# Loading queries, keys and values of the first eight attention tiles in fewer, longer transfers, with a planner that counts the places for transfers

## The chip, the cores and the metric

The kernel runs on one core of a Trainium2 chip. The metric is device time in microseconds (us), from one launch. Before the change, three runs took 1085.28, 1087.08 and 1091.06 us; the median is 1087.08 us. A profile was taken of one further execution.

The engines are named as in the profile: PE is the matrix engine (PEld its weight loads), DVE the vector engine, ACT the scalar engine, POOL the GpSimd engine and SP the one that issues most DMA transfers.

## The reference

Chunked attention over 4 batches, 8 heads, 768 tokens and 64 dimensions is followed by two feed-forward layers over the same 3072 tokens.

```python
# attention: 24 chunks of 32 queries; keys are 16 before, the chunk, 8 after, and 8 memory keys
k_full = np.concatenate([mem_k, k_ctx], axis=2)
v_full = np.concatenate([mem_v, v_ctx], axis=2)
scores = scale * np.matmul(q_c, k_full.transpose(0, 1, 3, 2))
a = np.exp(scores - np.max(scores, axis=-1, keepdims=True))
a = a / (np.sum(a, axis=-1, keepdims=True) + 1e-09)
out[:, :, c_start:c_end] = np.matmul(a, v_full)

# layer 1 on x [3072, 512], w_in [512, 2048], w_out [2048, 512]
h = x @ w_in
g = np.maximum(h, 0.0) + np.log1p(np.exp(-np.abs(h)))
x = (g @ w_out).astype(np.float32)
# layer 2, the same shapes
h = x @ w_in
g = np.maximum(h, 0.0) + alpha * np.minimum(h, 0.0)
out = (g @ w_out).astype(np.float32)
```

The weights come in as 64-bit floats (in_w_dram) and are made into 32-bit ones on the chip.

## The kernel before

**The tiles.** Attention is cut into 24 tiles of 128 tokens with all 8 heads. For a tile, the host lays out one block of 128 rows and 1664 floats: 1024 floats of Q, in which each head's 64 columns stand beside 64 zeros for the other head of the pair, and 640 floats of K (4 head pairs of 160 keys; the 8 memory keys stand at place 88 of each 160). Another block holds V as 96 rows of two halves of 512 floats.

**A block of work of layer 1** is either `h i` (12 matrix products of 128x512, which give one 128-wide slice of the hidden layer for 512 tokens) or `out i` (12 products which add that slice into the layer's output). The 512 tokens of four tiles are one batch b. Step i has a batch and a slice f; steps 0 to 3 are batch 0 with slices 0 to 3, steps 4 to 7 batch 1 with the same slices, and new slices begin again with step 8. So h 0 needs tiles 0 to 3, and h 4 needs tiles 4 to 7.

**The first eight tiles** (numbers 0 to 7, `t < 2 * TB`) are computed before and between the first blocks. One tile goes through: load Q and K (`load_q` twice, `load_k`), copy the memory keys to both ends of K on POOL (`a_mem`, name `km`), scores on PE (`a_scores`, name `s`, 32 small products), maximum, shift and exponent (`m`, `c`, `e`), sum, reciprocal and share (`n`, `r`, `w`), transpose on PE (`t`), copies on ACT (`pt`), values on PE (`v*`, 16 products), and a split of the result in two parts for exact products (`xh` on ACT, `xl` on DVE). For tile t, V is loaded by `load_v` in six transfers: two halves of 512 floats, each in pieces of 8, 56 and 64 rows.

**The weights** come as transfers `raw n` of 512 KB into three buffers. Five DVE instructions (`ab`, `cl`, `ca`, `cb`, `cv`) turn one into 32-bit floats; `wh` on ACT and `wl` on DVE split it in two parts. Slice f needs two of them.

**The order.** A planner (class `Plan`) takes each piece of work with an engine, a cost in us, a due time and what it comes after, and lays them out on all engines in one pass; the program is then written out in that order, and each engine does its instructions in that order. In the kernel before, the order of the opening is also written out by hand (`OPENING`), and due times come from a table of numbers `O`. A transfer costs the planner its issue on SP, its time on one resource "DMA" and 1.4 us more until its data may be used. All SP transfers go through eight places that are taken in turn: each transfer's issue waits until the one eight before it has landed.

**Filler.** `keep_busy` puts products with a tile of zeros into PE's queue ahead of a piece for which the planner sees PE wait early in the run; they change nothing in the result. The first of them fill the time before the first scores.

Of the kernel before, what the change touches and what calls it, by code (L numbers as in the profile page):

```python
# [35 lines left out]

VLATER = (
# [30 lines left out]
class InOrder:  # L68
# [5 lines left out]
    def __getattr__(self, name):  # L74
# [17 lines left out]
OPENING = {
    "": """
        qr 0, qr 1, qr 2, qr 3, vr 0, vr 1, vr 2, vr 3, qr 4, qr 5, vr 4, qr 6, vr 5, qr 7, vr 6, vr 7, qr 8, vr 8
    """,
    "DVE": """
        corners, m 0, c 0, m 1, n 0, c 1, r 0, w 0, n 1, r 1, m 2, w 1, c 2, ab 0, m 3, cl 0, c 3, n 2, ca 0, r 2, cb 0, w 2, ab 1, n 3, xl 0, r 3, cl
        1, w 3, cv 0, ca 1, ab 2, cb 1, wl 0, xl 2, cv 1, cl 2, ca 2, wl 2, cb 2, cv 2, xl 1, wl 1, xl 3, m 4, c 4, ab 3, cl 3, n 4, ca 3, r 4, cb 3,
        ab 4, lo 0, cv 3, lo 1, m 5, wl 4, c 5, ab 5, cl 4, cl 5, ca 4, cb 4, n 5, xl 4, r 5, cv 4, m 6, ca 5, c 6, cb 5, wl 3, n 6, cv 5, r 6, m 7, c
        7, wl 6, ab 6, cl 6, ca 6, cb 6, n 7, lo 2, r 7, cv 6, xl 5, wl 5, ab 7, cl 7, ca 7, cb 7, ab 8, cv 7, cl 8, xl 6, lo 3, wl 8, xl 7, ca 8, ab  # L100
        9, cb 8, cl 9, cv 8, ab 10, ca 9, cl 10, cb 9, wl 7, cv 9, lo 4, ca 10, wl 10
    """,
    "SP": """
        i q 0 0, i q 1 0, i q 0 1, i q 1 1, i qk 0 2, i qk 1 2, i cst, i q 2 0, i q 3 0, i q 2 1, i q 3 1, i qk 2 2, i qk 3 2, i v 2, i raw 0, i v 0,
        i raw 1, i v 3, i raw 2, i v 1, i q 4 0, i q 4 1, i qk 4 2, i q 5 0, i v 4, i q 5 1, i raw 3, i qk 5 2, i raw 4, i q 6 0, i v 5, i q 6 1, i
        raw 5, i qk 6 2, i q 7 0, i v 6, i q 7 1, i qk 7 2, i v 7, i raw 6, i q 8 0, i q 8 1, i qk 8 2, i v 8, i raw 7, i raw 8, i raw 9, i raw 10, i
        raw 11, i raw 12
    """,
    "POOL": """
        km 0, km 1, km 2, km 3, km 4, km 5, w 4, km 6, w 5, km 7, w 6, km 8, w 7  # L110
    """,
    "PE": """
        s 0, s 1, s 2, t 0, s 3, t 1, v* 0, t 2, v* 2, t 3, v* 1, v* 3, s 4, h 0, h 1, s 5, t 4, out 0, v* 4, s 6, h 2, s 7, t 5, out 1, t 6, v* 5, h
        3, v* 6, t 7, out 2, v* 7, h 4, h 5, out 3
    """,
    "ACT": """
# [6 lines left out]
class Plan:  # L123
# [18 lines left out]
    def run(self):  # L142
# [12 lines left out]
        while left:  # L155
            able = []
            for name, since in ready.items():
# [4 lines left out]
                if engine == "SP":  # L162
                    t = max(t, free.get("DMA", 0.0) - 4.0)
# [1104 lines left out]
```

## Time and profile before

| | us |
|---|---|
| runs: median (lowest to highest) | 1087.08 (1085.28 to 1091.06) |
| the profiled execution, whole | 1090.2 |
| its span, first to last instruction | 1088.1 |
| PE busy in the span | 1066.2 |
| DVE busy | 704.4 |
| ACT busy | 543.1 |
| POOL busy | 171.8 |

The profiled execution is 3.1 us above the median of the runs, and 2.1 us of it lie outside the span. An engine's busy time is the union of its instructions; a busy PE can be at either of its two clocks. A timeline row gives the start and the duration of instructions that follow each other with the same line, operation and tiles, and in brackets how long the engine stood idle before them and what released it. All helpers are recorded at line 76, so rows are told apart by their tiles.

### The profile page before, as it was taken

The numbers are of one execution on the slowest core, as the hardware profiler recorded it, in microseconds if no ns is written. First come the engines' busy times: TensorE is split into PE (matmuls) and PEld (weight loads), VectorE is DVE, ScalarE is ACT, GpSimd is POOL, SyncE is SP. The second block draws the span as 40 slices with busy tenths as digits, with TensorE's granted clock in tenths as the row PEclk, the third lists the DMA queues.
The fourth block names the chain that finished last, engine by engine and source line by source line (L and its number), as shares of the span: only waits on it lengthen the run. The fifth ranks groups of instructions, "written<-read, shape, count | busy, mean of one in ns | idle before, by whom it ended". The sixth has DMA issues, their size and how long they took to land.

```text
span 1088.1 us, 18751 instructions
## 1 busy us (share of the span) xinstructions
PE 1066.2 (98%) x7281; PEld 871.0 (80%) x7281; DVE 704.4 (65%) x1182; ACT 543.1 (50%) x940; POOL 171.8 (16%) x213
## 2 busy tenths in 40 slices
PE   6799999999999999999999999999999999999998
PEld 4568888778888888888888888888888888888886
DVE  5789988655554564345455156678666779566976
ACT  4564435455453454444344255664555755456643
POOL 0010112434234233222323100000000010000000
PEclk9989999999999999999999999999999999999999
DMA  8885674767656564535355173799875999856904
GB/s 203 209 188 182 188 196 126 187 184 192 197 165 183 175 170 128 187 120 166 111 180 191 61 288 126 282 282 322 200 280 174 327 298 256 259 203 256 372 0 78
DMA packets 156441, 214.69 MB, mean 197 GB/s; under 512 B 78656, under 2 KB 108480, under 8 KB 149440
## 3 DMA queue, kind: packets, MB, share of 16 engines
q1 hardware_dynamic: 152048, 196.58, 56.9%
q0 software_dynamic: 4032, 16.78, 8.1%
q8 instruction: 57, 0.93, 0.4%
q14 instruction: 32, 0.26, 0.1%
q10 hardware_dynamic: 272, 0.13, 0.0%
HBM read 154.74 MB, written 46.14 MB: 185 GB/s over the span
## 4 chain that ended last, share of the span: by engine, by line
PE 92%; DMA 5%; SPq 2%; DVE 1%; issue 0%; DVEq 0%
PE ps_q L76 42%; PE ps_hh L76 23%; PE ps_o L76 23%; PE ps_a L76 3%; DMA raw<-in_w_dram 3%; SPq L76 2%; DMA v<-in_v_dram 1%; DVE word L76 1%; DMA qk<-in_qk_dram 0%; DVE x L76 0%; DVE g L76 0%; DVE sm L76 0%; DVE wsplit L76 0%; DVE v L76 0%; DVE c L76 0%
## 5 line engine op out<-in xcount | busy, mean ns | idle before, releaser
L76 PE MATMUL ps_hh<-x,wsplit 128*128 128x512 f32 x1152 | 282.5, 394 | 1.9 <-DVE x L76 1.1
L76 PE MATMUL ps_o<-g,wsplit 128*128 128x512 f32 x1152 | 280.4, 392 | 0.8 <-DVE g L76 0.8
L76 PEld LDWEIGHTS ps_hh<-x,wsplit 128*128 128x128 f32 x1152 | 216.7, 189 | 49.0 <-DVE x L76 1.6
L76 PEld LDWEIGHTS ps_o<-g,wsplit 128*128 128x128 f32 x1152 | 214.3, 188 | 46.0 <-DVE g L76 1.1
L76 PE MATMUL ps_q<-xop,win 128*128 128x512 f32 x1008 | 229.1, 389 | 0.0
L76 PE MATMUL ps_q<-g,wout 128*128 128x512 f32 x1008 | 229.1, 389 | 0.0
L76 PEld LDWEIGHTS ps_q<-g,wout 128*128 128x128 f32 x1008 | 189.0, 188 | 39.5
L76 PEld LDWEIGHTS ps_q<-xop,win 128*128 128x128 f32 x1008 | 189.2, 188 | 39.3
L76 DVE TENSOR_TENSOR g<-ta,g 128x512 fp32r<-128x512 f32 x96 | 70.9, 738 | 132.5 <-ACT g L76 132.2
L76 ACT CAST g<-gb 128x512 fp32r<-128x512 f32 x168 | 100.8, 622 | 89.8 <-PE ps_q L76 66.1
L76 DVE TENSOR_TENSOR g<-gb,g 128x512 fp32r<-128x512 f32 x168 | 114.2, 686 | 35.2 <-ACT g L76 33.2
L76 ACT CAST g<-ta 128x512 fp32r<-128x512 f32 x96 | 59.6, 621 | 120.8 <-PE ps_o L76 120.6
L76 ACT ACTIVATE ta<-ps_hh 128x512 f32<-128x512 f32 x96 | 57.5, 599 | 119.8 <-PE ps_hh L76 116.5
L76 DVE SCALAR_TENSOR_TENSOR word<-raw,word 128x512 int32<-128x512 int32 x128 | 91.5, 715 | 2.7
L76 ACT ACTIVATE tp<-gb 128x512 f32<-128x512 f32 x48 | 30.4, 633 | 91.4 <-DVE gb L76 91.4
L76 POOL TENSOR_TENSOR wst<-wsum,wst 128x512 fp32r<-128x512 f32 x32 | 45.0, 1406 | 127.0 <-ACT wst L76 121.3
L76 DVE SCALAR_TENSOR_TENSOR gb<-gb,tp 128x512 f32<-128x512 f32 x48 | 33.2, 692 | 44.0 <-ACT tp L76 44.0
L76 DVE TENSOR_SCALAR word<-word 128x512 f32<-128x512 f32 (+1 forms) x128 | 57.3, 452 | 2.1
L76 POOL TENSOR_TENSOR wst<-word,wst 128x512 fp32r<-128x512 f32 (+1 forms) x32 | 34.2, 1068 | 140.3 <-ACT wst L76 135.1
L76 DVE TENSOR_SCALAR word<-raw 128x512 int32<-128x512 int32 x64 | 30.0, 471 | 39.8 <-DMA raw<-in_w_dram 26.9
L76 ACT ACT_TABLE_LOAD x38 | 48.8, 1283 | 11.1 <-DVE nm L76 10.5
L76 POOL DMA_DIRECT2D gb<-gb x12 | 10.4, 864 | 277.3 <-DVE g L76 168.4
(87 smaller groups left out, 860.6 us busy)
## 6 DMA issues: line engine op xcount, KB each, us to landing
wout<-out_ops SPq DMA_DIRECT2D x42, 1024.0 KB
raw<-in_w_dram SPq DMA_DIRECT2D x64, 512.0 KB
win<-in_ops SPq DMA_DIRECT2D x24, 1024.0 KB
win<-in_ops SPq DMA_DIRECT2D x24, 768.0 KB
out_ops<-wst SPq DMA_DIRECT2D x56, 256.0 KB
in_ops<-wst SPq DMA_DIRECT2D x24, 512.0 KB
gb<-gb POOLq DMA_DIRECT2D x12, 1024.0 KB, 13.7
qk<-in_qk_dram SPq DMA_DIRECT2D x24, 320.0 KB
```

Of the source, the lines that this page charges most:

```text
L76: i = getattr(self.engine, name)(*args, **kw)
```

## The change

Q and K of tiles 0 to 7 are loaded as whole rows of 1664 floats by one transfer in place of three (the zeros are then loaded too). V of these tiles is loaded by six transfers in two groups of three: 56 rows of both halves at once (runs of 4 KB), and twice 8 rows of one half. The order of the V rows in a tile changes with it. The memory keys are no longer copied; instead, for the first and the last chunk of a tile, `a_scores` makes two products in place of one, one of 56 keys and one of the 8 memory keys, so that a tile has 48 small products in place of 32.

In the planner, the written order `OPENING` is gone, as is the rule that SP runs at most 4 us ahead of the DMA. Each SP transfer takes one to four of eight places ("lane"), which come back when it has landed. Many costs are set anew, the wait after a transfer is 1.8 us, and work that follows work on the same engine starts 0.02 us after it rather than 0.15 us. The table `O` has other numbers, and `keep_busy` fills nine tenths of a wait, less 0.2 us, where it filled six tenths, less 0.5 us.

```diff
+FEW = KW - NMEM
+WINDOWS = (((0, 0, FEW), (FEW, MEM0, NMEM)), ((0, CHUNK, KW),), ((0, 2 * CHUNK, KW),), ((0, MEM0, NMEM), (NMEM, KT - FEW, FEW)))
+VFIRST = (
+    ((0, FEW, 0, None), (FEW, NMEM, MEM0, 0), (FEW, NMEM, FEW, 1)),
+    ((D + NMEM, FEW, SW - FEW, None), (D, NMEM, CHUNK, 0), (D, NMEM, MEM0 - D, 1)),
+)
...
-OPENING = {
...
-                if engine == "SP":
-                    t = max(t, free.get("DMA", 0.0) - 4.0)
...
-                if t < 90.0 and t - free.get("PE", 0.0) > 0.5:
+                if t < 90.0 and t - free.get("PE", 0.0) > 0.4:
...
-                    ready[a] = max(done[b] for b in left[a][4]) + self.LAG
+                    e = left[a][0]
+                    ready[a] = max(done[b] + (0.02 if e and e != "DMA" and self.pieces[b][0] == e else self.LAG) for b in left[a][4])
...
+    def load_rows(t):
+        sp.dma_start(out=rows_of[t][:, :QK], in_=qk[t])
...
-    def load_v(t):
+    def load_v(t, h):
         if t < 2 * TB:
-            for u, to, at, n in (
-                (0, 0, MEM0, NMEM), (0, NMEM, 0, KW - NMEM), (0, KW, CHUNK, KW),
-                (1, 0, 0, KW), (1, KW, SW - KW + NMEM, KW - NMEM), (1, 2 * KW - NMEM, MEM0 - D, NMEM),
-            ):
-                part = slice(u * DM, (u + 1) * DM)
-                sp.dma_start(out=v_t[t][to:to + n, part], in_=v[t][at:at + n, part])
+            for to, many, at, u in VFIRST[h]:
+                part = slice(0, 2 * DM) if u is None else slice(u * DM, (u + 1) * DM)
+                sp.dma_start(out=v_t[t][to:to + many, part], in_=v[t][at:at + many, part])
...
-                        pe.matmul(
-                            ps[at:at + CHUNK, g, u, :], lhsT=q[rows, u * NPAIR + g, c * CHUNK:(c + 1) * CHUNK],
-                            rhs=k_t[t][rows, g, KEYS[j]:KEYS[j] + KW], start=True, stop=True,
-                        )
+                        for to, key, many in WINDOWS[j]:
+                            pe.matmul(
+                                ps[at:at + CHUNK, g, u, to:to + many], lhsT=q[rows, u * NPAIR + g, e, c * CHUNK:(c + 1) * CHUNK],
+                                rhs=k_t[t][rows, g, key:key + many], start=True, stop=True,
+                            )
...
-                     "acc": 4, "y": 6, "w": NF, "x": 2})
+                     "acc": 4, "y": 6, "w": NF, "x": 2, "lane": 8})
...
-            add(name, "", 1.4, due, nothing, [("x",) + name], [], give)
+            add(name, "", 1.8, due, nothing, [("x",) + name], [], list(give) + lanes)
...
-            for e in range(2):
-                dma(("q", t, e), 0.66, 0.67, soon, lambda e=e: load_q(t, e), [("i", "q", t, 0) if e else ("qr", t)])
-            dma(("qk", t, 2), 0.65, 1.4, soon, lambda: load_k(t), [("i", "q", t, 1)])
...
+            else:
+                dma(("qk", t, 2), 0.42, 2.75, soon, lambda: load_rows(t), [("qr", t)])
...
-            spare[name] = max(0, int((until - since - 0.5) * 0.6 / 0.22))
+            spare[name] = max(0, int((until - since - 0.2) * 0.9 / 0.22))
```

SP, the transfers that stand last before the eighth tile's Q and K are in. Before; qk_528 and qk_623 are tiles 6 and 7, v_529 and v_624 the V of tiles 5 and 6:

```order
L76 DMA qk_528<-in_qk_dram 64x8x64
L76 DMA raw<-in_w_dram 128x512
L76 DMA qk_528<-in_qk_dram 128x4x160
L76 DMA qk_623<-in_qk_dram 64x8x64
L76 DMA v_624<-in_v_dram 8x512
L76 DMA v_624<-in_v_dram 56x512
L76 DMA v_624<-in_v_dram 64x512 x2
L76 DMA v_624<-in_v_dram 56x512
L76 DMA v_624<-in_v_dram 8x512
L76 DMA qk_623<-in_qk_dram 64x8x64
L76 DMA qk_623<-in_qk_dram 128x4x160
```

After; qk_551 and qk_650 are tiles 6 and 7, v_534 and v_550 the V of tiles 4 and 5:

```order
L82 DMA v_534<-in_v_dram 56x1024
L82 DMA v_534<-in_v_dram 8x512 x2
L82 DMA v_534<-in_v_dram 56x1024
L82 DMA v_534<-in_v_dram 8x512 x2
L82 DMA qk_551<-in_qk_dram 128x1664
L82 DMA raw<-in_w_dram 128x512
L82 DMA v_550<-in_v_dram 56x1024
L82 DMA v_550<-in_v_dram 8x512 x2
L82 DMA v_550<-in_v_dram 56x1024
L82 DMA v_550<-in_v_dram 8x512 x2
L82 DMA qk_650<-in_qk_dram 128x1664
```

Tile 7's row transfer now stands behind six tiles' V and four raw transfers; before, the last of its three stood behind seven tiles' V and six raw transfers.

PE, from tile 7's scores to the first block that needs tile 7 (h 4). Before; v_529, v_624 and v_702 belong to tiles 5, 6 and 7; behind these rows come four products with zeros, and then h 4 and h 5:

```order
L76 MATMUL ps_s<-qk_623 32x64 x32
L76 MATMUL ps_t<-cst,v_529 128x128 x4
L76 MATMUL ps_o<-g,wsplit 128x512 x12
L76 MATMUL ps_t<-cst,v_624 128x128 x4
L76 MATMUL ps_x<-pt,v_529 64x64 x16
L76 MATMUL ps_hh<-x,wsplit 128x512 x12
L76 MATMUL ps_x<-pt,v_624 64x64 x16
L76 MATMUL ps_t<-cst,v_702 128x128 x4
L76 MATMUL ps_o<-g,wsplit 128x512 x12
L76 MATMUL ps_x<-pt,v_702 64x64 x16
```

After; v_550, v_649 and v_819 belong to tiles 5, 6 and 7, the x36 row is h 3, h 4 and h 5:

```order
L82 MATMUL ps_t<-cst,v_649 128x128 x4
L82 MATMUL ps_o<-g,wsplit 128x512 x12
L82 MATMUL ps_x<-pt,v_550 64x64 x16
L82 MATMUL ps_hh<-x,wsplit 128x512 x12
L82 MATMUL ps_x<-pt,v_649 64x64 x16
L82 MATMUL ps_t<-cst,v_819 128x128 x4
L82 MATMUL ps_o<-g,wsplit 128x512 x12
L82 LDWEIGHTS zero
L82 MATMUL ps_x<-zero 128x512
L82 MATMUL ps_x<-pt,v_819 64x64 x16
L82 MATMUL ps_hh<-x,wsplit 128x512 x36
L82 MATMUL ps_o<-g,wsplit 128x512 x12
```

Before, seven blocks (h 0 to h 3, out 0 to out 2) stand ahead of h 4; now six do (h 0 to h 3, out 0 and out 1), of which two (h 0, h 1) stand ahead of tile 7's scores, where it was four. In the whole program the products with zeros are 66, where they were 41; the longest run of them is 19, ahead of tile 3's transposes.

## Rows read from the trace of the kernel before

**Rows 1.** The page, busy time of each engine and its share.

```profile
PE 1066.2 (98%) x7281; PEld 871.0 (80%) x7281; DVE 704.4 (65%) x1182; ACT 543.1 (50%) x940; POOL 171.8 (16%) x213
```

**Rows 2.** Stretches: length; busy by engine; PE clock, DMA share, GB/s.

```profile
37.34:77.15 39.81, 33.91 (x434) 25.78 (x428) 30.19 (x64) 24.51 (x42) 6.40 (x12) 0.96 0.89 210
77.15:84.11 6.96, 6.96 (x24) 5.59 (x24) 6.23 (x14) 2.36 (x4) 0.00 (x0) 0.75 0.41 118
160.00:640.00 480.00, 479.30 (x4038) 393.66 (x4038) 250.22 (x411) 215.48 (x340) 145.32 (x166) 1.00 0.54 161
```

**Rows 3.** Waits of PE from 77 to 640 us: total, times, longest.

```profile
PE ps_hh L76 <- DVE x L76: 1.1, 1, 1.1
PE ps_a L76 <- DMA v<-in_v_dram: 0.7, 1, 0.7
```

**Rows 4.** Timeline, tile 7 from its keys to h 4 and out 3.

```profile
58.72 0.67 POOL L76 COPY qk<-qk 128x32 f32<-128x32 f32 x2 [2.88 <-DMA qk<-in_qk_dram]
...
59.30 1.12 PE L76 MATMUL ps_s<-qk 64*32 64x64 f32 x64 [0.41 <-POOL qk L76]
...
63.95 0.63 ACT L76 ACTIVATE v<-v 128x512 f32<-128x512 f32 x1
...
67.69 1.23 POOL L76 TENSOR_TENSOR v<-v,r 128x512 f32<-128x512 f32 x1 [0.32 <-DVE r L76]
...
72.63 1.15 PE L76 MATMUL ps_x<-pt,v 128*64 128x64 f32 x32
...
77.15 7.12 PE L76 MATMUL ps_hh<-x,wsplit 128*128 128x512 f32 x23 [1.10 <-DVE x L76]
84.11 2.88 PE L76 MATMUL ps_o<-g,wsplit 128*128 128x512 f32 x12
86.83 2.88 PE L76 MATMUL ps_hh<-x,wsplit 128*128 128x512 f32 x12
```

**Rows 5.** Stretches in which one kind of transfer moved, and two others.

```profile
2.50:4.50 2.00, 2.00 (x6) 0.72 (x5) 0.72 (x3) 0.00 (x0) 0.00 (x0) 1.00 0.77 174
6.00:8.00 2.00, 0.00 (x0) 0.00 (x0) 0.00 (x0) 0.00 (x0) 0.13 (x1) 1.00 1.09 335
...
24.00:25.00 1.00, 0.80 (x6) 0.69 (x7) 0.06 (x1) 0.13 (x1) 0.00 (x0) 1.00 0.99 244
...
69.00:71.00 2.00, 2.00 (x22) 1.72 (x19) 0.53 (x2) 1.96 (x4) 0.00 (x0) 1.00 1.00 381
44.00:48.00 4.00, 3.12 (x36) 2.35 (x26) 2.87 (x6) 1.78 (x4) 0.38 (x1) 1.00 0.33 64
2.00:58.70 56.70, 42.93 (x712) 29.17 (x709) 37.90 (x87) 29.33 (x73) 4.88 (x16) 0.91 0.93 213
```

**Rows 6.** Timeline of SP's issues: the first six, and around 44 us.

```profile
0.74 3.99 SPq L76 DMA_DIRECT2D qk<-in_qk_dram  x6
...
38.07 5.11 SPq L76 DMA_DIRECT2D v<-in_v_dram  x6
45.01 0.63 SPq L76 DMA_DIRECT2D qk<-in_qk_dram  x1
```

**Rows 7.** Stretches with the PE clock at half.

```profile
53.50:56.92 3.42, 3.42 (x52) 2.77 (x41) 3.27 (x9) 0.73 (x2) 1.31 (x1) 0.50 1.04 166
77.40:80.81 3.41, 3.41 (x9) 2.65 (x9) 3.41 (x9) 0.62 (x1) 0.00 (x0) 0.50 0.19 23
```

**Rows 8.** Stretches after PE has no more waits.

```profile
84.11:100.00 15.89, 15.89 (x72) 13.16 (x71) 14.91 (x30) 6.78 (x12) 0.00 (x0) 1.00 0.59 191
100.00:120.00 20.00, 20.00 (x90) 16.57 (x89) 19.50 (x40) 8.33 (x15) 0.00 (x0) 1.00 0.62 204
120.00:140.00 20.00, 20.00 (x90) 16.57 (x89) 19.52 (x39) 8.92 (x16) 3.75 (x4) 1.00 0.73 173
```

**Rows 9.** Timeline of PE, products with zeros at two clocks.

```profile
1.00 4.45 PE L76 MATMUL ps_s<-zero 128*128 128x512 bf16 x10 [1.00 <-POOL zero L76]
...
19.08 1.47 PE L76 MATMUL ps_x<-zero 128*128 128x512 bf16 x6
```

More of the change, by code (lines that the diff above doesn't have):

```diff
@@ L92 @@
-OPENING = {
[L93 to L116, printed above, removed]
-        e 0, e 1, pt 0, e 2, pt 1, e 3, xh 0, pt 2, wh 0, xh 2, wh 2, pt 3, xh 1, wh 1, xh 3, e 4, sp 0, hi 0, sp 1, hi 1, wh 4, pt 4, e 5, xh 4, wh
-        3, e 6, sp 2, wh 6, pt 5, e 7, hi 2, pt 6, xh 5, wh 5, sp 3, pt 7, xh 6, hi 3, wh 8, xh 7, wh 7, sp 4, hi 4, wh 10, sp 5
-    """,
-}
@@ L146, in run @@
         wants, then, ready = {}, {}, {}
-        text = {name if isinstance(name, str) else " ".join(str(k) for k in name): name for name in left}
-        first = {e: [text[" ".join(x.split())] for x in names.split(",")] for e, names in OPENING.items()}
         for name, piece in left.items():
@@ L185, in run @@
             del ready[name]
-            if name in first.get(engine, ())[:1]:
-                first[engine].pop(0)
             came = 0.0
@@ L378, in load_q @@
         rows = qk[t][part, :QN].rearrange("p (n e k) -> p n e k", e=2, k=D)[:, :, e]
-        sp.dma_start(out=raw_q[t][part].rearrange("p (n k) -> p n k", k=D), in_=rows)
+        sp.dma_start(out=raw_q[t][part], in_=rows)
     def load_k(t):
@@ L430, in a_scores @@
     def a_scores(t):
-        q = raw_q[t].rearrange("p (n k) -> p n k", k=D)
+        q = raw_q[t]
         if t < 2 * TB:
@@ L465, in a_max @@
                  apool.tile([P, SLOTS, 1], F32, tag="sm", name="sm", bufs=2))
-        for rows, w, at, on in ((slice(0, D), 0, slice(NMEM, NMEM + LEFT), i == 0),
-                                (slice(D, P), 1, slice(LEFT + CHUNK, LEFT + CHUNK + RIGHT), i == TPB - 1)):
+        near, far = (NMEM, LEFT + CHUNK) if few else (0, NMEM + LEFT + CHUNK)
+        for rows, w, at, on in ((slice(0, D), 0, slice(near, near + LEFT), i == 0),
+                                (slice(D, P), 1, slice(far, far + RIGHT), i == TPB - 1)):
             if on:
@@ L1006, in nothing, with dma @@
             pass
-        def dma(name, issue, move, due, work, after=(), take=(), give=(), eng="SP"):
-            add(("i",) + name, eng, issue, due, work, after, take)
+        def dma(name, issue, move, due, work, after=(), take=(), give=(), eng="SP", lanes=1):
+            lanes = ["lane"] * lanes if eng == "SP" else []
+            add(("i",) + name, eng, issue, due, work, after, list(take) + lanes)
             add(("x",) + name, "DMA", move, due, nothing, [("i",) + name])
-            add(name, "", 1.4, due, nothing, [("x",) + name], [], give)
+            add(name, "", 1.8, due, nothing, [("x",) + name], [], list(give) + lanes)
         for n, k in enumerate(order):
```

84 lines of the change are left out of this document (46 added, 38 removed).

## The prediction

> **What bounds the kernel now.** I read the busy times first, then the stretches, then PE's waits, then the timeline. PE is busy for 1066.2 of 1088.1 us [rows 1], so all that can be won is some 22 us, and the reader should look for where they are. From 77.15 us PE works without a gap, but for two waits of 1.1 and 0.7 us up to 640 us [rows 2, 3]. Between 37.34 and 77.15 us it was busy for 33.91 of 39.81 us [rows 2], and part of that was filler or half clock. So the end is set by when PE's unbroken run begins, and by how much of its work is done by then. I measure that by one number, the start debt: the start of a block less 2.72 us for each block already done, 2.72 us being the distance from out 3 to h 6 (84.11 to 86.83) [rows 4]. Out 3 is the tenth block: 84.11 - 9 x 2.72 = 59.6 us. If the change moves the debt by some us, it moves the end by as many, as long as PE does not wait later.
>
> The timeline shows what made the debt. Tile 7's keys land at 58.7: POOL had stood for 2.88 us waiting for that transfer [rows 4]. Then come the copy of memory keys, scores at 59.30, exponent at 63.95, share at 67.69, values at 72.63, and h 4, which waits for tile 7's last piece (DVE x), at 77.15 [rows 4]. So what precedes is a stretch bound by transfers, 2.0 to 58.7 us with the DMA engines busy for 0.93 of the time at 213 GB/s [rows 5], and after it a chain of 17.85 us from the scores to h 4.
>
> **The change part by part: transfers.** Bytes follow from the shapes. Q and K of a tile were 2 x 131 KB + 328 KB = 590 KB (here KB is 1000 bytes), and are 852 KB; V is 524 KB and a weight transfer 524 KB in both. Up to the eighth tile's K, before: 8 x 590 + 7 x 524 + 6 x 524 and 74 KB of constants = 11.6 MB. After, by the order on SP: 8 x 852 + 6 x 524 + 4 x 524 + 74 KB = 12.1 MB. So more bytes stand ahead of the same point, and only the rate can make it earlier.
>
> Rates: Q halves alone (runs of 256 bytes) 174 GB/s, K alone (640 bytes) 335, V alone (2 KB, few rows at a time) 244, weights alone (4 KB) 381 [rows 5]. Before, by these: 8 x (1.51 + 0.98) + 7 x 2.15 + 6 x 1.38 + 0.3 = 43.5 us, against the 56.7 us that it took from 2.0 to 58.7. Of the difference, 2.7 us is the stretch from 44 to 48 us, when SP, having issued V until 43.18, stood until 45.01 [rows 6] and the engines ran at a share of 0.33 [rows 5]. The remaining 54.0 us are 1.24 times the sum: several kinds in flight at once move slower than each alone.
>
> After: no row shows runs of 6.6 KB. They are bounded by V's 244 and the weights' 381 GB/s, 3.5 to 2.2 us a tile; I take K's 335, the nearest row (128 rows of the same buffer), 2.54 us. V in runs of 4 KB: 1.38 us at the weights' rate to 2.15 us at its own; I take 2.15, since it still goes to 56 and 8 rows at a time. Weights 1.38. Sum: 8 x 2.54 + 6 x 2.15 + 4 x 1.38 + 0.2 = 38.9 us. The factor for mixing lies between 1.0 and 1.24; I take 1.15, since the short runs that are slowest are gone. So tile 7's keys land at 2.0 + 44.7 = 46.7 us, in place of 58.7; the factor's ends give 40.9 and 50.2. The stall at 44 us I expect to shrink: eight places now hold more bytes, since a row transfer is 852 KB, and fewer weight transfers, which wait for DVE to free a buffer, stand ahead of tile 7.
>
> [...]
>
> SP's issues: six for Q and K of two tiles took 3.99 us at the start [rows 6]; now it is two. That brings the first scores earlier, and is worth nothing by itself, since h 0 waits for V and weights further down the queue.
>
> **Copies and scores.** The memory copies go: scores began 0.58 us after POOL's copy did [rows 4]; now 0.3 us after landing, so tile 7's scores start at 47.0. They are 48 products in place of 32. The 64 records of 32 products took 1.12 us [rows 4]; 96 would take 1.68 at the same time each, and 1.12 if the narrow ones were free; I take 1.4.
>
> [...]
>
> **From the scores to h 4.** Before, 17.85 us (59.30 to 77.15) [rows 4], of which PE's own work was some 14.7 us: scores 1.12, three transposes at 0.66, two outs and one h at 2.72, three values at 1.15. After, PE has two h, as h 2 and h 3 both come behind the scores: 1.4 + 2 x 0.66 + 4 x 2.72 + 3 x 1.15 = 17.05 us. The chain is as long as before without the copy, and now work fills it almost fully, so both interleave; I take 17.85 + 1.5 = 19.3. So h 4 starts at 66.3, with six blocks done ahead of it: start debt 66.3 - 6 x 2.72 = 50.0 us. Before it was 59.6, in which the half clock from 77.40 to 80.81 us, 3.41 us of PE work [rows 7], had cost 1.7. PE still has gaps, so I charge one such stretch again, 1.7 us, though it could be none or two (before, another lay at 53.50 [rows 7]). Debt 51.7, rounded with 0.3 us for tile 5's and 6's scores to 52.0.
>
> **The rest.** After the opening the same blocks and the same 16 later tiles follow in another interleaving, with PE's waits at 1.8 us in all before [rows 3]; I cost that at zero, between -1.5 and +1.5. DVE covers it: it must have each weight split in time. The last layer is untouched.
>
> **Sum.** 59.6 - 52.0 = 7.6 us off. The profiled execution was 1090.2, so 1082.6 of the same kind; the median of the runs stands 3.1 lower at 1087.1, so 1079.5 us. Its own range, by the two landings (40.9 and 50.2), with work on PE setting a floor for the early one, is 1075 to 1083.
>
> **Rivals.**
> *Same bytes per us.* If 213 GB/s [rows 5] is what the queue gives whatever the runs, 12.14 MB take 57.0 us, tile 7 lands at 59.0, h 4 starts at 59.3 + 19.3 = 78.6, the debt is 62.3 + 2.0 = 64.3, and the kernel is slower by 4.7 us: 1091.8. Place: SP's queue ahead of tile 7's rows; it decides from a landing after 54.3. For it: a share of 0.93 says the engines were not idle. Against it: 335 and 381 GB/s in the same stretch with other runs [rows 5].
> *DVE takes over.* From 100 to 140 us DVE is busy 39.0 of 40 us [rows 8]. Tile 7's move ahead of two weight transfers puts the two conversions, with some 2.8 us of DVE each, behind h 4, into a time in which PE runs 7.6 us earlier and DVE has 1 us in 16 to spare. If PE then waits for weights for 4 us in all, the gain is 3.6: 1083.5. Against it: PE had not one wait for weights there [rows 3], and four of the blocks behind h 4 use no new weights.
> *Filler in the way.* 66 products with zeros for 41. At half clock one takes 0.44 us, else 0.25 [rows 9]; the 19 ahead of tile 3's transposes are 4.7 us, or 8.4. If the clock is down there, 3.7 us pass to all that stands behind on PE: gain 3.9, 1083.2.
>
> **How the numbers follow.** My forecast 0.60, DVE 0.20, filler 0.08, same bytes 0.12. 0.5% (5.4 us, to 1081.7) is about what a measurement of this kernel tells from no change. Faster by more: 0.88 of the first, a fifth of the second and third, 0.59 in all. Slower by more than that, over 1092.5, would need the last rival at worse than its price or with filler on top, and a cause not listed: 0.08. Within: 0.33. The range: 1074 (landing at 40.9 with no half clock) to 1088 leaves out most of the slow rival and no more.
>
> **What would show it.** Right: tile 7's scores at 45 to 50 us, Q and K rows moving above 300 GB/s where they are alone, out 3 with nine blocks or more ahead and a start debt of 50 to 54, no POOL copies before 50 us, and PE without gaps from about 65. Wrong: scores of tile 7 later than 54 us; PE waits on DVE's weights between 100 and 190 us; a run of zeros that ends after the DVE piece it was to wait for. DMA shares near 1 with rates near 213 GB/s would show the slow rival.

## The result: 1.4% slower, and the opening no earlier

The changed kernel took 1104.08 us (median of four runs, 1100.81 to 1105.13), the kernel before 1087.62 us (median of four runs, 1085.28 to 1091.06). The ratio is 1.0144, 95% interval 1.0108 to 1.0179: 16 us slower. The profiled execution has a span of 1103.4 us, against 1088.1; it stands 1.1 us above the median of its runs, that of the kernel before 2.6 us above. PE's busy time on the page of the changed kernel, for [rows 1]:

```profile
PE 1072.4 (97%) x7562; PEld 875.4 (79%) x7562; DVE 715.8 (65%) x1182; ACT 541.6 (49%) x940; POOL 168.9 (15%) x197
```

PE is busy only 6 us longer, so most of the 15.3 us is standing still. PE's longest waits in the changed kernel over the whole span (total, times, longest), for [rows 3]:

```profile
PE ps_q L82 <- ACT tc L82: 12.7, 1, 12.7
PE ps_s L82 <- issue: 4.4, 1, 4.4
PE ps_t L82 <- issue: 3.5, 2, 3.1
```

The first wait is one event, at the start of layer 2, behind the stretch of [rows 3]; the kernel before has no wait there. The next two are named "issue": PE stood, and nothing that the profile shows held it. The timeline of PE in the changed kernel shows where: before the last of tile 1's four transposes (and the eleven products with zeros behind it), in the middle of tile 5's scores, then tile 7's scores, out 3 (for [rows 4]), the last block of layer 1 and the start of layer 2.

```profile
20.89 0.37 PE L82 MATMUL ps_t<-cst,v 128*128 128x128 f32 x1 [3.12 <-issue]
21.05 3.87 PE L82 MATMUL ps_x<-zero 128*128 128x512 bf16 x11
...
37.82 0.78 PE L82 MATMUL ps_s<-qk 64*32 64x56 f32 x45
43.03 1.46 PE L82 MATMUL ps_s<-qk 64*32 64x8 f32 x51 [4.43 <-issue]
...
56.86 1.46 PE L82 MATMUL ps_s<-zero 128*128 128x512 bf16 x6 [1.61 <-DVE x L82]
58.26 1.37 PE L82 MATMUL ps_s<-qk 64*32 64x56 f32 x96
...
86.41 2.88 PE L82 MATMUL ps_o<-g,wsplit 128*128 128x512 f32 x12
...
628.36 2.88 PE L82 MATMUL ps_o<-g,wsplit 128*128 128x512 f32 x12
643.95 73.07 PE L82 MATMUL ps_q<-xop,win 128*128 128x512 f32 x312 [12.71 <-ACT tc L82]
```

Ten blocks stand ahead of out 3 here, so the start debt is 86.41 - 27.2 = 59.2 us: what it was before (59.6), not 52.0. Each debt is read from one execution, and the first experiment below, with the same order in its opening, has out 3 at 84.17 us: a difference of some 2 us between two such debts tells little. In the kernel before, the last block of layer 1 and the start of layer 2 are

```profile
628.24 2.88 PE L76 MATMUL ps_o<-g,wsplit 128*128 128x512 f32 x12
630.96 70.88 PE L76 MATMUL ps_q<-xop,win 128*128 128x512 f32 x312
```

So up to layer 1's last block the two kernels are level. Behind it come 12.71 us of waiting in the changed kernel, and the next 312 products take 73.07 us instead of 70.88, since PE ran the first of them at half clock (granted clock 0.50 from 643.95 to 647.00 us, shown further down). That is 14.9 of the 15.3 us.

**Layer 2's start.** These rows of the changed kernel are ACT's and POOL's, around that wait:

```profile
621.55 0.62 ACT L82 CAST wst<-word 128x512 fp32r<-128x512 f32 x1
628.39 0.41 ACT L82 CAST wst<-word 128x256 fp32r<-128x256 f32 x1 [6.22 <-DMA in_ops<-wst]
...
641.89 0.62 ACT L82 CAST wst<-wsum 128x512 fp32r<-128x512 f32 x1 [4.30 <-DMA out_ops<-wst]
...
643.32 1.06 ACT L82 COPY tc<-ps_q 128x512 f32<-128x512 f32 x2
...
642.58 2.50 POOL L82 TENSOR_TENSOR wst<-wsum,wst 128x512 fp32r<-128x512 f32 x2 [3.72 <-ACT wst L82]
```

`wst` holds the second layer's weights, split ahead of time and stored for later (a cast on ACT, a subtraction on POOL, a store). ACT has eight of these casts left after 621 us (three are shown), five of them waiting for an earlier store to free a buffer, and `tc`, which empties PE's first results of layer 2, is queued behind them. In the kernel before, the last of this work was

```profile
607.86 1.29 POOL L76 TENSOR_TENSOR wst<-wsum,wst 128x512 fp32r<-128x512 f32 x1 [1.34 <-ACT wst L76]
...
624.36 0.59 ACT L76 COPY tc<-ps_q 128x512 f32<-128x512 f32 x1 [3.40 <-PE ps_q L76]
```

35 us earlier, and ACT stood idle for 3.40 us until PE gave it `tc`.

**The transfers** did become faster. Stretches of the changed kernel (columns as in [rows 2]): rows of Q and K alone; the second stop; what follows it; a stretch behind tile 7's rows; the start of layer 2.

```profile
3.20:4.80 1.60, 0.54 (x2) 0.00 (x0) 0.12 (x1) 0.00 (x0) 0.00 (x0) 1.00 1.02 424
38.60:43.02 4.42, 0.00 (x0) 0.00 (x0) 2.08 (x5) 1.16 (x2) 1.04 (x1) 0.75 1.00 236
44.00:48.00 4.00, 4.00 (x25) 3.13 (x19) 3.13 (x7) 1.84 (x2) 0.00 (x0) 0.55 0.82 249
51.00:56.00 5.00, 4.25 (x48) 3.49 (x48) 4.72 (x9) 3.24 (x6) 0.00 (x0) 1.00 0.04 16
...
643.95:647.00 3.05, 3.05 (x7) 2.47 (x8) 2.66 (x4) 1.15 (x3) 1.13 (x1) 0.50 0.75 244
```

Whole rows move at 424 GB/s, and from 51 to 56 us the DMA engines stand: all that had been issued is in, tile 7's rows too. The trace's packet records give the landing itself: the last packet of the eight row transfers ended at 46.7 us, where the last one of tile 7's keys ended at 57.55 us before. Yet tile 7's scores run at 58.26 us, only a microsecond earlier than before (59.30, [rows 4]). PE was late, not the data: it came through its queue to these scores at 55.25 us, stood 1.61 us until DVE's split of an earlier tile (`x`) was done, and then ran six products with zeros.

### The profile page after: what moved, and what is told of

Its sections match the earlier page's. It is cut to its first block, busy times and chain, and to the rows that moved or that the text cites. A ratio compares the mean times of both kernels' runs of the same rounds, so it can differ in the third digit from the quotient of the medians.

```text
span 1103.4 us, 19256 instructions
## 1 busy us (share of the span) xinstructions
PE 1072.4 (97%) x7562; PEld 875.4 (79%) x7562; DVE 715.8 (65%) x1182; ACT 541.6 (49%) x940; POOL 168.9 (15%) x197
## 4 chain that ended last, share of the span: by engine, by line
PE 94%; DMA 2%; DVE 2%; issue 1%; POOL 1%; ACT 1%; SPq 0%; DVEq 0%; POOLq 0%; ACTq 0%
PE ps_q L82 41%; PE ps_hh L82 23%; PE ps_o L82 23%; PE ps_a L82 3%; PE ps_s L82 1%; DVE word L82 1%; PE ps_x L82 1%; DMA in_ops<-wst 1%; PE ps_t L82 1%; DMA raw<-in_w_dram 0%; DMA qk<-in_qk_dram 0%; POOL wst L82 0%; DMA out_ops<-wst 0%; POOL wsum L82 0%; DVE sm L82 0%
## 5 line engine op out<-in xcount | busy, mean ns | idle before, releaser
L82 PE MATMUL ps_o<-g,wsplit 128*128 128x512 f32 x1152 | 277.4, 392 | 0.0
L82 PE MATMUL ps_hh<-x,wsplit 128*128 128x512 f32 x1152 | 276.7, 393 | 0.0
L82 PE MATMUL ps_q<-xop,win 128*128 128x512 f32 x1008 | 231.3, 392 | 12.7 <-ACT tc L82 12.7
L82 DVE TENSOR_TENSOR g<-ta,g 128x512 fp32r<-128x512 f32 x96 | 75.5, 787 | 147.8 <-ACT g L82 147.8
L82 ACT CAST g<-ta 128x512 fp32r<-128x512 f32 x96 | 59.7, 622 | 30.2 <-PE ps_o L82 28.4
L82 POOL TENSOR_TENSOR wst<-wsum,wst 128x512 fp32r<-128x512 f32 x32 | 42.7, 1337 | 145.2 <-ACT wst L82 145.2
L82 DVE TENSOR_SCALAR word<-raw 128x512 int32<-128x512 int32 x64 | 27.6, 431 | 27.3 <-DMA raw<-in_w_dram 19.9
## 6 DMA issues: line engine op xcount, KB each, us to landing
gb<-gb POOLq DMA_DIRECT2D x12, 1024.0 KB, 13.5
```

Source lines behind the costliest of these rows:

```text
L82: i = getattr(self.engine, name)(*args, **kw)
```

## The experiments

Two theories were to be tested. A: the planner laid the second layer's weight preparation out too late, and that alone is the wait of 12.7 us. B: the bursts of small products (96 a tile instead of 64) use PE's instructions up faster than they are fetched, and that is the stops named "issue". From here on small products are counted as the trace records them: the program's 48 products for a tile's scores are 96 records, and its 32 before were 64.

### Old costs for the second layer's conversions

```diff
-            add(("ab2", j), "DVE", 0.43, due - 1, ...
-            add(("cl2", j), "DVE", 0.43, due, ...
-            add(("cv2", j), "DVE", 1.84, due, ...
+            add(("ab2", j), "DVE", 0.35, due - 1, ...
+            add(("cl2", j), "DVE", 0.34, due, ...
+            add(("cv2", j), "DVE", 1.55, due, ...
```

> The changed kernel with one thing put back: the planner counts the three conversion pieces of the second layer's weights at their old costs on VectorE (0.35, 0.34 and 1.55 us instead of 0.43, 0.43 and 1.84). The opening's order is the same to the last instruction; the order of layer 1's middle and of the second layer's weight preparation changes. Theory A (the planner lays the preparation out past the end of layer 1, so that ScalarE still holds its last casts when layer 2 wants its first operand): TensorE's one wait of 12.7 us at 644 us and the 2.2 us at half clock behind it go, 1104 - 15 = 1089 us (1087 to 1092), the last weight sum on GpSimd ends by 600 us. Rival (the preparation is late because the stores themselves are slow, whatever the order): wait of 10 us or more stays, 1101 to 1105 us. Both: the first stretch up to out 3 is unchanged, out 3 at 86.4 us (within 0.7).

1093.35 us, ratio to before 1.0058 (1.0040 to 1.0076). The wait at layer 2 is gone, as A says; the last row of `wst` pieces on POOL begins at 602.99 us and ends at 605.5 (A had 600). Out 3 missed too: 84.17 us, where 86.4 within 0.7 was expected of an unchanged order. The time is 1.4 us above A's range, for a reason that A did not have: in the new order PE stops at 250 us, where 128 small products stand in a row, and waits once more for ACT.

```profile
84.17 2.88 PE L82 MATMUL ps_o<-g,wsplit 128*128 128x512 f32 x12
...
251.87 5.63 PE L82 MATMUL ps_hh<-x,wsplit 128*128 128x512 f32 x24 [2.17 <-issue]
...
265.05 0.49 PE L82 MATMUL ps_o<-g,wsplit 128*128 128x512 f32 x1 [2.12 <-ACT g L82]
...
602.99 2.54 POOL L82 TENSOR_TENSOR wst<-wsum,wst 128x512 fp32r<-128x512 f32 x2 [4.72 <-ACT wst L82]
```

### One product for each window

```diff
-                        for to, key, many in WINDOWS[j]:
-                            pe.matmul(ps[at:at + CHUNK, g, u, to:to + many], ..., rhs=k_t[t][rows, g, key:key + many])
+                        pe.matmul(ps[at:at + CHUNK, g, u, :], ..., rhs=k_t[t][rows, g, AT[j]:AT[j] + KW])
...
+    kf = np.concatenate([kf[..., :FEW], kf[..., MEM0:SW], kf[..., CHUNK:2 * CHUNK + KW], kf[..., MEM0:SW], kf[..., KT - FEW:]], axis=3)
```

> The changed kernel with 64 products for a tile's scores again instead of 96, and still no copies of memory keys: the host lays the keys of the first eight tiles out as the four windows one behind the other (224 columns a head pair instead of 160), so a row is 7.7 KB instead of 6.6 KB, in one transfer. Filler and planner costs stay. Theory B (bursts of small products use up TensorE's instructions faster than they are fetched): the two stops of TensorE without a releaser, 3.1 us at 17.8 and 4.4 us at 38.6, shrink to under 1 us each, and out 3 begins at 78 to 81 us instead of 86.4. Rival B' (the long rows on the DMA engines hold up the fetch of instructions): stops of 3 to 4 us stay, out 3 at 85 to 88 us. In both the whole time hardly follows, since layer 2 still waits for its weights: 1098 to 1106 us; only with an earlier preparation would the gain show.

1098.92 us, ratio 1.0104 (1.0078 to 1.0130). Out 3, and the stops:

```profile
80.08 2.88 PE L84 MATMUL ps_o<-g,wsplit 128*128 128x512 f32 x12
...
PE ps_q L84 <- ACT tc L84: 11.9, 1, 11.9
PE ps_s L84 <- DMA qk<-in_qkf_dram: 5.3, 5, 2.0
PE ps_t L84 <- issue: 3.1, 2, 1.7
```

The stops fall from 7.9 to 3.1 us and out 3 comes 6.3 us earlier (4.1 us against the first experiment's 84.17), although the rows grew: theory B, not its rival. Of this, 8 x 0.27 = 2.2 us are the products' own time (a tile's 64 take 1.10 us, 96 take 1.37). The two stops that the expectation named are gone, but two others of 1.34 and 1.74 us stand elsewhere, longer than the 1 us that it allowed. I expected the gain not to show in the whole; it did, since the preparation moved forward with the rest and layer 2 waited 11.9 us.

### Both

> The edits of the two runs before together: old costs for the second layer's conversions, and one product for each window from host-laid windows. Theories A and B: 1104 - 15 - 7 = 1082 us (1079 to 1085). A with the rival B' (long rows hold up the fetch): 1088 to 1091 us. The rival of A with B: 1098 to 1105 us.

1088.99 us, ratio 1.0016 (1.0000 to 1.0032): not the 1082 of A and B. The opening did as expected (out 3 at 80.28 us, debt 53.1, no stop named "issue" ahead of it), and layer 2 did not wait. The opening's order is that of the run before, which had 3.1 us of stops and an out 3 at 80.08 us: there the stops cost nothing that shows, as PE without them waited longer for its rows (6.7 us here, 5.3 there). What is missing went at 247 us, in the same place as in the first run, and this time with half clock behind it (7.12 us for 24 products instead of 5.63):

```profile
247.30 7.12 PE L84 MATMUL ps_hh<-x,wsplit 128*128 128x512 f32 x24 [2.18 <-issue]
```

With two waits of 0.26 and 0.33 us behind it that makes 4.3 us. The profiled executions bear the sum out: 14.9 us at layer 2 and 6.1 us in the opening, less 4.3, are 16.7 of the 17.5 us between the spans of the changed kernel (1103.4) and of this run (1085.9).

### The kernel before, with 96 products a tile

```diff
-                        pe.matmul(ps[at:at + CHUNK, g, u, :], ..., rhs=k_t[t][rows, g, KEYS[j]:KEYS[j] + KW])
+                        for to, many in (((0, KW - NMEM), (KW - NMEM, NMEM)), ((0, KW),), ((0, KW),), ((0, NMEM), (NMEM, KW - NMEM)))[j]:
+                            pe.matmul(ps[at:at + CHUNK, g, u, to:to + many], ..., rhs=k_t[t][rows, g, KEYS[j] + to:KEYS[j] + to + many])
```

> The kernel before, its loads and order as they were, with the first and the last window of each of the first eight tiles computed as two products (56 and 8 columns) on the same data, so 96 products a tile instead of 64. Theory B (instruction supply, by the number of small products): stops without a releaser appear on TensorE in the first 45 us, 3 us or more in all (before 0.3), and out 3 is later by 3 to 7 us, 1090 to 1095 us. Rival B' (long rows hold up the fetch): no stop above 0.6 us, a tile's scores take 1.37 us instead of 1.12, out 3 later by 0 to 1.5 us, 1087 to 1089 us.

1088.36 us, ratio 1.0002 (0.9982 to 1.0022). `KW` is 64 and `NMEM` 8. The stops appear with the old transfers too, so long rows are not needed for them; the number of products is:

```profile
14.66 1.21 PE L76 MATMUL ps_s<-qk 64*32 64x64 f32 x83 [0.99 <-issue]
...
19.95 0.92 PE L76 MATMUL ps_s<-qk 64*32 64x8 f32 x56 [2.62 <-issue]
```

They are 3.6 us where the changed kernel has 7.9, and here they cost nothing that shows: out 3 began at 82.08 us, not later than before (84.11), since PE stood 8.3 us there in waits for POOL's copies, that is for keys still in transit, and a stop takes the place of such a wait. So B was right on the stops and missed on out 3 and on the time, which came out as the rival had it. By this run a stop costs where the data are already there.

### The supply of instructions by itself

The loop, shortened, with comments that are not in the kernel:

```diff
+    for phase in range(3):
+        ...   # phase 2: 16 transfers of whole rows; phase 3: the same bytes in short runs
+        warm(40)                          # zero products of 512 columns
+        products(ps, rooms[0], 720)       # 64x32 by 64x64, from a resident row
```

> Not the computation of the reference: a kernel that measures the supply of TensorE's instructions by itself (its output is a block of left-over numbers). Three phases, each 40 zero products of 512 columns (about 9 us, full clock) and then 784 small products of the scores' size (64 rows by 32, 64 columns) one behind the other, which need nothing but the first 720's resident row. Phase 1: no transfers run. Phase 2: sixteen transfers of whole rows of 6.6 KB run beside it. Phase 3: the same bytes as the kernel before loads them (256 bytes and 640 bytes a piece). Theory B (small products use instructions up faster than they are fetched, and a busy set of DMA engines makes the fetch late): phase 1 runs with short stops or none, 14 to 18 ns a product; phases 2 and 3 stop for 1 us or more every 128 to 350 products. Rival B' (it is the long rows that hold the fetch up): stops of that size in phase 2 alone. Rival B'' (the supply itself is the limit, whatever else runs): phase 1 stops as much as phase 2.

Its rows, the first stops of each phase (no transfers; whole rows; short runs). The 784 products of a phase are 1568 records:

```profile
49.30 2.76 PE L82 MATMUL ps_a<-room 64*32 64x64 f32 x181
53.50 1.99 PE L82 MATMUL ps_a<-room 64*32 64x64 f32 x128 [1.45 <-issue]
56.96 1.99 PE L82 MATMUL ps_a<-room 64*32 64x64 f32 x128 [1.47 <-issue]
...
102.44 3.53 PE L82 MATMUL ps_b<-room 64*32 64x64 f32 x235
109.60 1.99 PE L82 MATMUL ps_b<-room 64*32 64x64 f32 x128 [3.62 <-issue]
115.79 3.64 PE L82 MATMUL ps_b<-room 64*32 64x64 f32 x128 [4.21 <-issue]
121.99 5.44 PE L82 MATMUL ps_b<-room 64*32 64x64 f32 x256 [2.56 <-issue]
...
168.62 2.47 PE L82 MATMUL ps_c<-room 64*32 64x64 f32 x161
173.89 1.99 PE L82 MATMUL ps_c<-room 64*32 64x64 f32 x128 [2.79 <-issue]
178.44 2.66 PE L82 MATMUL ps_c<-room 64*32 64x64 f32 x128 [2.56 <-issue]
183.81 3.64 PE L82 MATMUL ps_c<-room 64*32 64x64 f32 x128 [2.71 <-issue]
```

After the first run of 161 to 235 products PE stops after every 128 (a few times after 181 or 256). In the quiet phase, from 53.50 to 88.00 us, the queue named "instruction" moved 10 packets of 16 KB for 1280 products:

```profile
q8 instruction: 10, 0.16, 1.8%
```

That is one packet for 128 products, each of which has a weight load of its own (1279 products and 1280 loads are recorded in that stretch). The sustained pace is (88.00 - 53.50) / 1280 = 27 ns a product with the DMA engines idle (a share of 0.02), against 1.99 / 128 = 15.5 ns while instructions last; (121.99 - 102.44) / 491 = 40 ns beside whole rows and (188.64 - 168.62) / 545 = 37 ns beside short runs. So B as it was put missed in the quiet phase, where it had short stops or none, and B'' holds in part: the supply is a limit by itself (stops of 1.45 to 2.0 us). Beside traffic the stops are longer: 2.6 to 4.2 us beside whole rows (3.5 on average) and 1.2 to 2.8 beside short runs (2.3), against 1.7 on average in the quiet phase. Parts of both phases ran at half clock, as the 3.64 us for 128 products show (mean granted clock 0.81 from 102.44 to 122 us and 0.76 from 168.62 to 190).

The trace's packet records show where the time goes. In the quiet phase the packet of 16 KB begins 0.3 to 1.2 us before PE runs out of work (at 54.6 us, for example, with PE's run ending at 55.5), and PE goes on some 1.4 us behind the packet's end. Beside whole rows it begins 1.3 and 1.6 us after PE has stopped, in the two longest stops (107.3 and 113.2 us, with runs that ended at 106.0 and 111.6), and again PE goes on 1.2 to 1.6 us behind its end. The longest stop of the changed kernel looks the same: PE stops at 38.60 us, the packet begins 1.6 us later and takes 1.3 us, and PE goes on 1.6 us behind it. So in these stops the fetch begins late, beside DMA engines that are full (a share of 1.00 from 38.60 to 43.02 us in the changed kernel, 1.02 from 102.44 to 122 us here).

### Lower conversion costs, and less filler

The first of these two takes the run with both edits and sets the three costs to 0.33, 0.32 and 1.45; the second does in addition

```diff
-            spare[name] = max(0, int((until - since - 0.2) * 0.9 / 0.22))
+            spare[name] = max(0, int((until - since - 0.5) * 0.6 / 0.22))
```

> The run with both edits (one product for each window; old conversion costs in the planner) with the three conversion costs a little lower still (0.33, 0.32 and 1.45 us), which gives another order of layer 1's middle; the opening is the same. That run lost 4.3 us at 247 to 261 us: 2.2 us in a stop without a releaser behind 128 small products in a row, 1.5 us at half clock behind it and 0.6 us in two waits. Theory B (the stop comes where a run of small products meets a late fetch, so that the order decides): without that stop 1082 us (1080 to 1085); with one like it 1086 to 1089 us. Rival (something in the change itself costs layer 1's middle 4 us whatever the order): 1086 to 1090 us without any such stop in sight.

> As the run beside it (one product a window, lower conversion costs), with the filler of the opening by the formula of the kernel before ((gap - 0.5) x 0.6 / 0.22 zero products instead of (gap - 0.2) x 0.9 / 0.22). Theory C (the filler takes TensorE after its operands are there, so it delays the opening): out 3 begins 1 to 3 us earlier than in the run beside it, and the whole is 1 to 3 us shorter. Rival (the filler lies in real gaps; what bounds the opening is the chain of scores, VectorE and transfers): out 3 within 0.7 us, the same time within 0.2%, or up to 3 us longer where TensorE falls to half clock.

1085.02 us, ratio 0.9986 (0.9970 to 1.0002), and 1084.17 us, ratio 0.9967 (0.9953 to 0.9981). In the first, the stop at 247 us is gone, though the same 128 products stand in a row at 244 us; in the changed kernel 128 stand in a row at 256 us without a stop too. So a run of that length does not always bring one; that it depends on where in the stream the fetch falls is a reading, which no run here tests. But another wait took its place (2.11 us at 207.80 us, for DVE's `x`), again with half clock behind it (4.58 us for an out block instead of 2.88). So neither answer to the first run's question was right as put.

In the second run out 3 begins at 78.97 us instead of 80.44, as theory C says; the whole is shorter by 0.85 us (0.2%), just under its 1 to 3. The place is ahead of tile 7's scores. In the first of the two runs PE stood there for DVE and then still had six products with zeros to do, for 1.4 us, with its operands there (the last packet of the rows ended at 49.5 us); in the second there are three.

```profile
51.14 1.46 PE L84 MATMUL ps_s<-zero 128*128 128x512 bf16 x6 [1.61 <-DVE x L84]
```

### The landing cost, and the places

```diff
-            add(name, "", 1.8, due, nothing, [("x",) + name], [], list(give) + lanes)
+            add(name, "", 1.4, due, nothing, [("x",) + name], [], list(give) + lanes)
```

and, in the other run,

```diff
-            lanes = ["lane"] * lanes if eng == "SP" else []
+            lanes = []
```

> The changed kernel with one other number put back: the planner counts 1.4 us instead of 1.8 us from a transfer's move to its landing. The conversion costs stay as changed. In the planner's own order the last store of the second layer's split weights is then issued 5 us behind the start of layer 1's last output block; in the changed kernel it is 31 us behind, in the run with the old conversion costs 18 us ahead of it. Theory A (how far the planner laid the preparation out behind layer 1's end decides, whichever cost did it): no wait of TensorE over 2 us between 620 and 660 us. Rival A' (the conversion costs themselves, or the stores, make layer 2 wait): a wait of 8 us or more stays. The opening changes too (stops without a releaser 4 to 9 us in all, as there are 96 products a tile): 1088 to 1098 us by A, 1100 us or more by A'.

> The changed kernel with the planner's count of eight places for transfers left out; all costs stay. Its own order has the last store of the second layer's weights 17 us behind the start of layer 1's last output block, between the changed kernel (31 us) and the run with the shorter landing (5 us). Theory A: TensorE's wait at the start of layer 2 lies between 0 and 6 us, shorter than the 12.7 us of the changed kernel. Rival A' (the wait does not follow the distance laid out): 8 us or more. 1088 to 1100 us by A.

1092.21 us, ratio 1.0041 (1.0014 to 1.0068), without any wait at layer 2's start (its stops named "issue" are 7.8 us in all, one of 3.2 us before 251 us); and 1090.51 us, ratio 1.0025 (1.0001 to 1.0049), with a wait of 2.22 us:

```profile
627.84 2.52 POOL L82 TENSOR_TENSOR wst<-wsum,wst 128x512 fp32r<-128x512 f32 x2 [3.72 <-ACT wst L82]
...
629.19 71.04 PE L82 MATMUL ps_q<-xop,win 128*128 128x512 f32 x312 [2.22 <-ACT tc L82]
```

Five orders now stand in a row. The last row of `wst` pieces on POOL begins 14.2 us behind layer 1's last block in the changed kernel (642.58 and 628.36), 13.5 us with one product a window (635.88 and 622.39), 3.8 us without places (627.84 and 624.09), 5.8 us ahead of it with the shorter landing (624.22 and 630.01), and 27.9 ahead in the first experiment (602.99 and 630.86); layer 2 waits 12.7, 11.9, 2.2, 0 and 0 us. That is theory A, and no single cost is to blame. The planner makes eight plans and takes the one whose layer 1 ends first; where the preparation ends has no part in the choice.

### No filler in the gaps, and two counter-checks

```diff
-            spare[name] = max(0, int((until - since - 0.5) * 0.6 / 0.22))
+            spare[name] = 0
```

in three kernels: the run with less filler; the kernel before; and the changed kernel with 96 products and the lower conversion costs (where the line taken out is the changed kernel's, with 0.2 and 0.9). The filler ahead of the very first scores stays in all three.

> The run with less filler (one product a window, lower conversion costs) with no zero products at all in the opening's gaps but those ahead of the first two tiles' scores that start the clock. Theory C (every zero product that outlasts its gap delays the opening): out 3 begins another 0.5 to 1.5 us earlier than in that run (78.97 us), 1082 to 1084 us. Rival (the zero products keep TensorE at full clock): more stretches at half clock in the first 60 us, out 3 0.5 to 4 us later, 1084 to 1089 us.

> The kernel before with no zero products in the opening's gaps but those ahead of the first scores. It asks whether the gain of the last run (1081.8 us: one product a window, lower conversion costs, no filler) is the filler's alone. Theory D (most of that gain is the change's own loads and the memory copies that are gone): this kernel stays within 1.5 us of before, 1085.5 to 1088.5 us. Rival D' (leaving out the filler is the gain): 1081 to 1084 us.

> The changed kernel, with its 96 products a tile and its own rows of 6.6 KB, with the two later edits alone: the lower conversion costs and no filler in the gaps. So it is the run that was fastest, with the first and the last window split again. Theory B (96 small products a tile outrun the fetch of TensorE's instructions): stops without a releaser of 3 to 8 us in the first 60 us, out 3 at 82 to 86 us (78.4 with 64 products), 1085 to 1090 us. Rival E (without the zero products, which are instructions too, the stops are gone and 96 products cost only their own time): stops under 1.5 us, out 3 by 80 us, 1081 to 1084 us.

The first took 1081.84 us, ratio 0.9948 (0.9926 to 0.9970): the fastest of all, and faster than before by an interval that lies wholly below 1. The rival was right that more of the opening would run at half clock (granted clock 0.50 from 28.4 to 35.2 us, where the run with less filler had 1.00), but out 3 came earlier all the same. Behind the products with zeros ahead of everything else, the first tile's scores ran at full clock in the profile of the kernel before (64 records in 1.12 us at 8.13 us), and here they did not (1.93 us at 5.60 and again at 8.43 us, 1.10 at 23.42). Its debt is 78.44 - 27.2 = 51.2 us; tile 7's scores wait for its rows, of 7.7 KB here, until 50.00 us:

```profile
50.00 1.08 PE L84 MATMUL ps_s<-qk 64*32 64x64 f32 x60 [2.42 <-DMA qk<-in_qkf_dram]
...
78.44 2.88 PE L84 MATMUL ps_o<-g,wsplit 128*128 128x512 f32 x12
```

The kernel before without filler took 1086.50 us, ratio 0.9999 (0.9982 to 1.0016), so the gain is not the filler's alone (theory D). Its one profile shows how little one execution tells: out 3 at 78.53 us with nine blocks ahead, a debt of 54.1 us against the 59.6 of the kernel before, and a span 5.0 us shorter, where ten runs show no gain. With 96 products the same edits gave 1085.48 us, ratio 0.9986 (0.9969 to 1.0003), out 3 at 81.59 us, and PE stopped three times:

```profile
26.38 0.92 PE L82 MATMUL ps_x<-pt,v 128*64 128x64 f32 x24 [1.79 <-issue]
...
35.49 1.97 PE L82 MATMUL ps_x<-pt,v 128*64 128x64 f32 x31 [1.64 <-issue]
...
41.32 4.55 PE L82 MATMUL ps_hh<-x,wsplit 128*128 128x512 f32 x12 [1.67 <-issue]
```

5.1 us of stops and an out 3 that is 3.2 us later: theory B again, out 3 just under its range, and not E. How much of the 3.2 us is the stops stays open: 2.2 us are the products' own time, and half clock lasted from 27.8 to 44.9 us here (granted clock 0.50), 17.1 us against 6.8 in the run with 64. By the two ratios the 32 extra products a tile cost 0.4% in all, about 4 us; with both intervals, an estimate of 1 to 7 us.

## Why the prediction was wrong, step by step

Two steps failed: the rest, put at zero, and the cost of splitting the scores.

- **"The rest", costed at zero, and "The last layer is untouched".** This step made the kernel slower: 14.9 of the 15.3 us. The last layer's instructions are unchanged, but they read weights which layer 1 prepares, and the planner's new costs moved that work across the border between the layers. It could have been seen beforehand, in the order of ACT around the end of layer 1, where casts for the second layer now stand ahead of `tc`; I looked at the opening alone.
- **Copies and scores, 1.4 us for 48 products.** This step took most of the gain away. The price of a tile's scores was right (1.37 us). What it left out is that 96 records in a row, with 32 or more small products close by, outrun the fetch (15.5 ns a record until a stop, 27 ns sustained, in the run of the supply by itself): 7.6 us in two stops, each with half clock behind it (granted clock 0.50 from 20.9 to 23.3 us, 0.55 from 44 to 48). The debt came out at 59.2 us, and with one product a window at 53.1, and 51.2 without filler, against my 52.0. These 6 us, from one execution of each kernel (4 us by the first experiment's), are the split's whole price in the opening, the products' own 2.2 us among them; they cannot be told apart further, since a stop costs only where PE would not have waited anyway (3.6 us of them cost nothing that shows in the kernel before with 96 products).
- **Transfers.** The landing of tile 7 was right: the last packet at 46.7 us, with some 1.2 us more before an engine may go on (before, 57.55 and 58.72), against a forecast of 46.7 for the latter. It was right in part by luck. Rows alone ran at 424 GB/s, above the 244 to 381 that I had as bounds, so that eight of them cost 16.1 us and not 20.3; the sum is then 34.7 us, and the 44.7 that passed are 1.29 times it, above my 1.0 to 1.24 for mixing. That PE would start on tile 7's scores 0.3 us after the landing failed: it came to them at 58.26 us, held up by the stops, by a wait for DVE and by filler. Without filler they waited for their rows, until 50.00 us, with rows a seventh longer.
- **From the scores to h 4, 19.3 us.** In the changed kernel h 3 begins at 72.66 us, so h 4 at about 75.4, 17.1 us after tile 7's scores; in the kernel without filler 64.71 and 67.4, 17.4 us after them. Somewhat too long, on the safe side.
- **Half clock.** One stretch, 1.7 us, was charged in the opening. The changed kernel had two there, behind the two stops, and lost about 3.5 us in them by an estimate from the same rows in the other runs: eleven products with zeros took 3.87 us (2.57 with one product a window), 51 of tile 5's records 1.46 (0.73 at full clock) and h 0 4.58 (3.1). A further 2.2 us went behind the long wait.
- **The rivals.** *Same bytes per us* is refuted by 424 GB/s and by the idle engines at 51 us. *DVE takes over* did not come: PE has no wait for weights behind the opening of the changed kernel. *Filler in the way* was right in kind and not in place: the 19 products ahead of tile 3's transposes ended 0.35 us before what they filled the time for, but those ahead of tile 7's scores took 1.4 us from PE when it could have gone on, and out 3 moved from 80.44 to 78.97 us with less filler and to 78.44 with none. None of them was the cause of the loss.
- **"Wrong" signs that I named.** The first came true, scores of tile 7 later than 54 us (58.26), but it was meant to tell of a late landing, and the landing was in time. None of the three says "a stop without a releaser" or "a wait at layer 2": I looked for trouble only where the change was made.

## What to carry to other kernels

When costs in a planner change, look at its order at every border that the work crosses, not only where the change is meant to act, and let the planner's choice count all ends that someone waits for (this was not tried here). Splitting one small product in two cost more than its time here (some 6 us of the opening, by one execution of each kernel, for 2.2 us of products): count a run of small products in the trace's records, and where a run is longer than 128 of them while transfers are running, look for a stop (some runs of 128 here had one, of 2.2 us, others none). Once such stops were gone, filler in the same queue was the next thing that delayed (out 3 from 80.44 us to 78.44 without it). And read a start from more than one execution before calling two kernels different: here one order of the opening gave 86.41 and 84.17 us.

## What the runs showed of the hardware

- The queue named "instruction" moved 16 KB for every 128 small products of PE (10 packets for 1280). A sequence of small products ran at 15.5 ns each until PE stopped, and at 27 ns in the long run with no other transfer, 37 to 40 ns beside traffic that filled the DMA engines (a share of 1.02 and more; partly at half clock, mean granted clock 0.81 and 0.76). Stops are 1.45 to 2.0 us in the first case and up to 4.2 us in the second.
- The stop shows in the profile as idle time released by "issue", and in the stop at 38.60 us of the changed kernel the DMA engines were busy for 1.00 of the time while PE did nothing. With no traffic its packet began 0.3 to 1.2 us before PE ran out, in the two longest stops beside whole rows 1.3 and 1.6 us after; PE went on 1.2 to 1.6 us behind the packet's end in both.
- Rows of 6.6 KB reached 424 GB/s where nothing else moved.
- Idle times of 2.1 us (at 208 us with lower conversion costs: 4.58 us for an out block behind it instead of 2.88), 2.2 us (at 247 us with both edits: 7.12 us for 24 products instead of 5.63) and 12.7 us (at 644 us in the changed kernel: granted clock 0.50 to 647.00 us) were followed by half clock, and so were the stops of 3.1 and 4.4 us in the changed kernel's opening (granted clock 0.50 from 20.9 to 23.3 and 0.55 from 44 to 48 us); one of 2.2 us at 250 us in the first experiment was not (24 products in 5.63 us, granted clock 1.00).
